# A sorted-block attention and Fourier-mix kernel: three more tile transposes by the DMA crossbar, GpSimd shares an elementwise step, one buffer clear moves, and a new written-out order

## The chip, the cores and the metric

The kernel runs on one core of one Trainium2 chip. The metric is the device time of one launch in microseconds (us). The kernel before the change took 272.64 us, the median of three runs (271.47 to 272.67).

The core has five instruction streams: PE (TensorE, the matmuls, with its weight loads listed as PEld), DVE (VectorE), ACT (ScalarE), POOL (GpSimd) and SP (SyncE, which here only issues DMAs). POOL computes and also issues the loads from HBM. All DMAs of the core, whoever issues them, share 16 DMA engines.

## What is computed

Inputs are q, k, v of shape (4, 8, 768, 64), a sort matrix (4, 8, 8, 8) and two weights (512 x 2048 and 2048 x 512), all float32. Cut to what matters:

```python
P = sinkhorn(sort_net)                      # 5 rounds: exp, row and column normalise
k_sorted = einsum("bhij,bhjcd->bhicd", P, k_blocks)     # 8 blocks of 96 rows
v_sorted = einsum("bhij,bhjcd->bhicd", P, v_blocks)
attn = softmax(q_block @ k_sorted_block.T / 8)
x = attn @ v_sorted_block                   # regrouped to (4, 768, 512)
u = x + real(fft(fft(x, axis=1), axis=2))
un = (u - mean(u)) / sqrt(var(u) + 1e-6)    # over the last axis
out = u + maximum(un @ w_ch1, 0) @ w_ch2
```

## The kernel before

**Tiling and stages.** The four batches run one after the other with much overlap. A batch b has eight heads (four pairs hp) and 768 rows, which are six tiles T of 128 rows. The rows are handled in two halves, g = 0 (tiles 0 to 2) and g = 1 (tiles 3 to 5). Each step is a small Python generator, named by a letter and its indices. The ones that matter here:

- `x` b hp g (L529, L534): scores of two heads on PE, then exp on ACT into an `ex` tile (96 x 384).
- `e` b hp g (L548): one instruction for each of the two heads writes exp minus 1 from `ex` into the padded buffer `eb`. All 64 are on DVE. There are four `eb` buffers.
- `o` b h (L561, L570, L575): attention times values on PE, the reciprocal and the scaling on DVE.
- `f`, `c` (L680 to L739): folds and the first Fourier product. `d` b T (L755, L758, L769): the second one, with two DVE steps into `u`. `p` b T (L776, L782, L784): a copy on ACT, then an add and a subtract on POOL (letter P) or DVE (letter D). `g` b T (L791, L795): mean and variance on DVE. `l` b g (L799 to L808): four small POOL steps that give `ny` and `nm`, the scale and the bias of a half.
- `n` b g tt (L816 or L819, then L825 or L830): the normalized rows `un` (128 x 512, f16, two buffers) by ACT or DVE, and then their transpose into `ut`. In batch 0 this is four PE transposes (L830) and one copy out of PSUM (L286 or L288); in batches 1 to 3 it is one crossbar transpose that SP issues (L825).
- `h` b g fc (L843, L850, L852): the first feed-forward product of a half, 16 groups of four matmuls, each of which reads all of `ut` of that half (128 x 384) and a slice of `w1sb`; then the relu by ACT or DVE.
- `y` b g tt n (L863, L868, L870): the second product, the addition of `u`, and the store by SP.
- `k`, `q`, `v`, `w`, `s`, `M`, `Z`, `a`, `A`, `R`, `r` prepare sorted keys and values, queries, and the correction terms of the transform. `I` issues two matmuls whose result nobody uses.
- `C0`'s steps after the first two have POOL issue the loads of `w1sb` (four, L362) and `w2sb` (four, L365). `L` has POOL load later q and k (L188).

**What sets the order.** A string `ORDER` lists the steps; each mention of a step runs its generator one `yield` further. At the end, every instruction of an engine is tied to the one before it on the same engine, so each of the five streams runs exactly in the written order, POOL's loads and SP's transposes and stores among them. An instruction that waits holds up all that stands behind it on its engine. The letters behind a step choose its engines. A second string, `SLOTS`, chooses the PSUM bank or the buffer of every tile.

In the order before, half g = 0 of batch 0 is normalized and goes through `h` first, and g = 1 later. Before the loop, DVE clears three of the four `eb` buffers (L246) and POOL the fourth (L258).

Of the kernel before, what the change touches and what calls it, by code (L numbers as in the profile page):

```python
# [18 lines left out]
H = 8  # L19
S = 768  # L20
D = 64
# [85 lines left out]
def kernel(  # L107
# [10 lines left out]
    nc = tc.nc  # L118
# [7 lines left out]
        "00011101 00010234 50671030 12436570 13541602 05240031 63725241 "  # L126
        "61012052 63475001 25314102 06103012 04513222 10030415 11274602 "
        "53130145 36510210 03210302 01560420 33200075 60111221 22340330 "
        "01276225 10173200 00200653 04210013 13610004 56102525 11621110 "
        "65112701 35471623 05243052 00016450 16110470 21112364 21160323 "  # L130
        "61172420 61372041 64161010 20345245 17630010 04176325 11271652 "
        "37261401 05032102 33560171 00310010 00620057 32036401 11017624 "
        "23213156 23520605 43101204 47051106 01110521 03411070 16502411 "
        "02713260 50732415 00274113 52224760 11003511 22104731 00001210 "
        "17315000 14236220 31041230 03107652 01103651 01547162 30400762 "
        "37631401 07521240 11101501 01641320 27614031 54302100 11023201 "
        "50262732 36000054 07001001 51143120 04353542 00117102 16572110 "
        "40111035 60270456 07453147 352041 "
# [27 lines left out]
    def start(ins):  # L166
        return tc.keep_in_program_order(ins)
# [74 lines left out]
    NE = 4  # L242
    eb4 = const.tile([97, NE, 2 * S], F16, name="eb4")
    ebuf = [eb4[:, n, :] for n in range(NE)]
    for n in range(NE - 1):
        nc.vector.memset(ebuf[n][0:96, :], 0.0)  # L246
# [11 lines left out]
    start(nc.gpsimd.memset(ebuf[NE - 1][0:96, :], 0.0))  # L258
# [261 lines left out]
    exs = {}  # L520
# [19 lines left out]
    def t_e(b, hp, g):  # L540
        for h2 in range(2):
            if h2:
                yield
            e = ebuf[(2 * hp + h2) % NE]
            ed = bass.AP(
                tensor=e.tensor, offset=e[:, S * g:S * g + 1].offset,
                ap=[e[0:96, :].ap[0], [224, 4], [1, BLK]])
            nc.vector.tensor_scalar(ed, exs[b, hp, g, h2], -1.0, None,  # L548
                                    op0=ALU.add)
# [261 lines left out]
    def t_n(b, g, tt, eng, e2="A"):  # L811
# [10 lines left out]
        if b > 0:  # L822
            if (b, g) not in uns:
                uns[b, g] = wt([128, 4, GT], F16, "ut", 2)
            nc.sync.dma_start_transpose(  # L825
                uns[b, g][:, :, 128 * tt:128 * tt + 128], un)
            return
# [52 lines left out]
    def t_i():  # L880
# [4 lines left out]
        "C0 I4 I5 M00 M01 M02 M03 J M04 M05 C0 B0 C1 B1 B2 D q00A Z0 "  # L885
        "Z0 s02 k00AA H k01AD Z0 s03 q00 k00 k00 k00 x001 k01 b0 s01 "
        "x000 x001 s04 b0 x000 x000 a0 a0 x001 s05 s00 q01D k01 q02D "
        "k01 k02AA q01 e001 k02 k02 v61A v61 v40A e001 v70A v40 v41D "
        "v50D a0 b1 k02 v41 q02 v30A v30 x010 V x010 x010 V T1 v70 "
        "v20A e010 v20 v50 e000 e000 e010 A0 R0 x011 x021 R0 R0 R0 "  # L890
        "q03D q03 R0 R0 x011 x011 x021 v60D v10A v60 v00A k10AA v10 "
        "e011 e011 x021 k03AA R0 v00 x020 x020 k03 k03 k03 o00 o01 "
        "k10 k10 k10 x020 e021 x030 o00 e020 x030 x030 e021 o02 o01 "
        "o00 o01 o03 o02 o03 x031 q11A r1 C2 C3 r0 r1 e030 o03 e020 "
        "o04 k11AA x031 e031 x031 o05 e030 R0 o04 e031 o04 q11 k11 R0 "
        "o02 o05 k11 q10A q13A q13 v51A o07 o07 o05 q10 v51 M10 o06 "
        "v31A k11 x111 x101 x101 x101 v31 M11 o07 o06 f00 o06 f00 "
        "v21A v01A f01 f01 k13AA e101 x110 f02 k13 f02 M12 M13 e101 "
        "f03 f03 M14 v21 x100 x111 x110 x111 e110 c00 L20 f04 x100 "
        "x110 c00 b1 L30 M15 C0 L20 q20 C0 f05 f05 Z1 v01 C0 e111 "  # L900
        "e110 c01 c01 c02 c00 e111 c01 c02 c03 c04 e100 r0 r0 v71A "
        "k12AA c03 q20 c04 d02 v71 v11A x100 d02 p02P d00 p02 d01 k12 "
        "q12A k12 e100 d00 c03 p00P p01P q12 v11 k13 d02 c04 d00 d01 "
        "Z1 c02 d04 p00 k12 k13 d01 p02 p01 p01 p04P Z1 I1 p00 d05 T2 "
        "g02 g01 p05P x121 x121 x131 x131 a1 o13 o10 a1 x121 g00 g01 "
        "x131 C0 g02 g00 l00 l00 l00 l00 e121 o12 I2 x130 e131 o11 "
        "d04 o12 d05 x130 x130 d05 d04 k20AA n001AA o11 q21 I3 e130 "
        "o11 d03 n001 n002AA n001 L21 n000DD o16 n002 p04 o12 n000 "
        "n000 L21 C0 p04 o16 p05 C0 n002 x120 x120 d03 k20 e130 p03P "
        "o13 s15 e120 o13 h00iA h00fD h00f h00i x120 o10 s10 o10 "  # L910
        "h00jD h00j e121 d03 h00cA h00pA h00hA h00h h00p q21 o16 "
        "h00dA e120 k21AA k21 s13 k21 k20 k20 h00c h00kD e131 s12 s14 "
        "x200 k21 h00oA h00nA s11 o14 x200 h00d x200 h00gA o17 h00aA "
        "h00k h00a h00lA wpA h00g p05 C0 o17 o17 o15 h00mA h00bA g05 "
        "o15 o14 o14 wkA h00l h00b wk h00n h00eA h00e o15 f10 h00o wp "
        "y0010 y0020 e200 g04 x201 x201 L30 x211 x211 p03 p03 g03 f11 "
        "f11 g04 f10 f12 h00m C0 g05 g03 l01 f12 e200 f13 y0021 y0022 "
        "l01 l01 x201 weD wbA wb wgD c10 we y0023 l01 q22 f13 n011DA "
        "e201 c10 f14 woA c11 c11 wo y0000 wjD e211 wj x211 y0001 "
        "n011 n011 c12 wg f15 whA wdA y0011 y0002 c13 c12 wh y0023 "  # L920
        "y0023 r1 n012DD f15 n012 y0012 wlA n012 c13 y0013 wcA q22 "
        "wnD waA wa n010DD n010 wl y0003 n010 wd c14 c14 h01aA wn "
        "y0003 wfD q23 q23 T3 y0013 c10 d11 h01oA h01o wiA h01dD h01d "
        "h01lA h01l y0003 y0013 d10 h01pA wc h01a wi h01p wf h01jD "
        "wmD h01gA wm e201 x210 d10 d10 c11 h01g x210 x210 p10P h01j "
        "d12 h01mA k22AD k22 k22 k22 e210 e210 k23DD q31 k23 k23 "
        "h01cA c13 d11 p12P h01c h01hA h01h p11P k23 h01fA h01f e211 "
        "h01iA d12 h01bD d12 p11 h01m h01i h01kA x230 x231 d11 h01b "
        "p12 p12 p11 g11 g12 g11 g12 x220 h01eA x230 h01e x220 x230 "
        "y0110 o22 x231 e231 o20 h01nD h01n o20 h01k o21 p10 p10 o23 "  # L930
        "o23 o20 L31 x220 L31 g10 g10 o23 y0111 y0112 y0120 a1 l10 "
        "l10 l10 l10 o22 o22 y0121 k31AA c14 n101A k31 q31 e230 e220 "
        "A1 c12 x231 o21 o21 k31 x221 n101 R1 e231 R1 n100A n100 "
        "y0100 y0101 q30 R1 R1 R1 n102A n102 x221 y0113 y0113 d13 "
        "y0102 y0122 R1 R1 e230 y0113 x221 e221 k31 d14 R1 R1 r2 r2 "
        "h10iA h10nA h10i d14 q30 k30DD e221 k30 k30 k30 y0123 r2 "
        "e220 y0123 p14P o27 h10eD h10n h10e h10kD o27 d14 y0123 "
        "y0103 d15 o27 h10aA h10a h10dA h10gA h10g h10bA y0103 h10k "
        "p13D p15P h10cA h10c h10hA h10mA h10m h10d q32 d13 d13 y0103 "
        "h10lA h10h h10jD p13 p14 p14 g14 d15 d15 g14 p15 p15 h10fA "  # L940
        "h10f h10oA o26 g15 p13 g13 g13 g15 l11 l11 l11 h10j o26 "
        "h10pD o26 h10b y1010 l11 o24 o24 y1000 h10l o25 n110D o25 "
        "h10o h10p y1011 x311 x311 x311 x301 f21 o25 f21 y1001 n112A "
        "x301 y1020 y1021 o24 f20 f20 n110 r3 e301 n111D y1002 y1012 "
        "f22 f22 f23 f23 c20 c20 y1013 y1022 q32 x300 x301 x300 x310 "
        "y1023 c21 c21 n112 f24 f25 c23 n111 e311 q33 y1013 y1023 c23 "
        "h11cD c22 f25 y1003 y1003 y1023 y1003 c22 c24 x300 h11c c24 "
        "k32DD k33DA k33 k33 e311 x310 k32 k32 d21 k33 p21P k32 d21 "
        "d21 e300 h11fD h11f h11oA e310 d22 d20 p20P h11lA p22P d22 "
        "d22 c24 h11mA c20 r3 h11kA q33 y1013 d20 h11l h11o p22 p22 "  # L950
        "h11m x310 h11hD h11jA h11j g22 o32 x331 e300 x331 h11bA p21 "
        "h11h x331 h11k g22 o32 h11eA h11iA e310 p20 c23 e301 p21 g21 "
        "h11b o32 h11pD h11aD h11a h11e h11i d20 p20 g20 g20 e331 "
        "x330 g21 l20 l20 l20 l20 h11p x321 h11gA h11g h11dA o31 x321 "
        "o30 o31 o31 e321 x321 h11nA h11d n202A y1110 x330 c22 o33 "
        "h11n y1111 y1112 n202 o33 e330 e331 c21 n201A o33 n201 n200D "
        "n200 r3 y1100 y1101 e321 x320 x320 e320 y1113 y1113 o30 "
# [84 lines left out]
```

## Time and profile before

One execution was profiled. Its own time and the main numbers:

| what | value |
| --- | --- |
| time of the profiled execution | 271.9 us |
| its span in the profile | 270.1 us |
| median of three runs | 272.64 us |
| PE busy | 251.8 us (93%) |
| DVE busy | 196.3 us (73%) |
| ACT busy | 126.0 us (47%) |
| POOL busy | 75.0 us (28%) |
| granted PE clock, mean | 0.994 |
| first `h` matmul starts | 61.84 us |
| last PE matmul ends | 267.4 us |
| crossbar transposes `ut<-un` | 18, median 2.4 us to landing |
| crossbar transposes `qt<-qr` | 8, 2.8 to 9.0 us to landing |

How to read it: the page gives busy time by engine, the span cut in 40 slices, the DMA queues, the chain of work that ended last, and groups of instructions by line. The trace behind it answers for single stretches: who waited for whom, instructions in order of time, busy time by stretch, and for each DMA the time from its issue to its landing. Times count from the span's start. A busy PE isn't PE at its peak, since matmuls are pipelined and their ends are modelled.

### The profile page before, as it was taken

What the parts mean: (1) busy time and instruction counts of PE and PEld (TensorE: products, weight loads), DVE (VectorE), ACT (ScalarE), POOL (GpSimd) and SP (SyncE); (2) the same over time, 40 slices, a digit from 0 to 9 for tenths busy, and PEclk for the clock granted to TensorE, in tenths of its full rate; (3) what the DMA queues carried; (4) which work ended last, traced back from release to release, by engine and by line L of the source; (5) the groups of instructions that cost most, each with busy time, mean ns of one, the idle gap of its engine ahead of it and who ended that gap; (6) DMA issues with size and microseconds to landing.
All of it is one profiled execution on the core that took longest, in us unless ns stands there. A gap on an engine that the chain in (4) does not pass through costs nothing.

```text
span 270.1 us, 6119 instructions
## 1 busy us (share of the span) xinstructions
PE 251.8 (93%) x2440; PEld 156.0 (58%) x2440; DVE 196.3 (73%) x489; ACT 126.0 (47%) x287; POOL 75.0 (28%) x118
## 2 busy tenths in 40 slices
PE   0789889789999999999999999999999999999995
PEld 0268776565666666655656655466466545545554
DVE  6787999989999677867698696458965825912523
ACT  2268889885575477352633555133314312431100
POOL 8922400578730006402220053024200521410000
PEclk9988999999999999999999999999999999999999
DMA  6999999989971231843022310230023023020006
GB/s 120 203 253 203 221 245 235 181 104 178 204 119 39 45 102 29 119 107 101 15 55 52 94 47 12 55 119 1 19 42 116 0 45 132 0 53 8 0 12 223
DMA packets 33138, 26.38 MB, mean 98 GB/s; under 512 B 17395, under 2 KB 28787, under 8 KB 33108
## 3 DMA queue, kind: packets, MB, share of 16 engines
q0 software_dynamic: 11712, 13.63, 30.4%
q1 hardware_dynamic: 21398, 12.36, 17.2%
q8 instruction: 19, 0.31, 0.5%
q14 instruction: 9, 0.07, 0.1%
HBM read 29.00 MB, written 6.29 MB: 131 GB/s over the span
## 4 chain that ended last, share of the span: by engine, by line
PE 77%; DVE 8%; DMA 8%; POOL 2%; ACT 2%; issue 1%; DVEq 0%; SPq 0%; POOLq 0%
PE pf L863 31%; PE pf L843 27%; DMA k<-in_k_dram 6%; PE pf L719 3%; PE pf L561 3%; PE pf L529 2%; DVE eb L548 2%; DMA out_dram<-u 2%; PE pf L755 2%; PE pf L758 1%; DVE u L769 1%; PE pf L486 1%; PE pf L511 1%; PE pf L476 1%; PE pf L615 1%
## 5 line engine op out<-in xcount | busy, mean ns | idle before, releaser
L843 PE MATMUL pf<-ut,w1sb 128*128 128x384 f16 x512 | 89.9, 326 | 0.4 <-DVE hr L850 0.2
L863 PE MATMUL pf<-w2sb,hr 128*128 128x512 f16 (+1 forms) x432 | 88.6, 355 | 0.0
L843 PEld LDWEIGHTS <-w1sb 128*128 128x128 f16 x512 | 48.7, 98 | 31.5 <-issue 0.4
L852 ACT ACTIVATE hr<-pf 128x384 f16<-128x384 f32 x78 | 35.8, 494 | 60.6 <-PE pf L843 60.5
L863 PEld LDWEIGHTS <-hr 128*128 128x128 f16 x432 | 38.5, 98 | 37.7
L782 POOL TENSOR_TENSOR u<-u,bs 128x255 f32<-128x255 f32 x21 | 17.6, 844 | 120.2 <-ACT bs L776 69.1
L868 DVE TENSOR_TENSOR u<-pf,u 128x512 f32<-128x512 f32 (+1 forms) x27 | 17.0, 628 | 29.0 <-PE pf L863 28.9
L534 ACT ACTIVATE ex<-pf 96x384 f32<-96x384 f32 x64 | 28.8, 490 | 10.6 <-PE pf L529 8.0
L850 DVE TENSOR_SCALAR hr<-pf 128x384 f16<-128x384 f32 x50 | 26.3, 547 | 7.7 <-PE pf L843 7.6
L548 DVE TENSOR_SCALAR eb<-ex 96x384 f16<-96x384 f32 x64 | 22.9, 374 | 2.6 <-ACT ex L534 2.4
L769 DVE SCALAR_TENSOR_TENSOR u<-r,pf 128x256 f32<-128x256 f16 x48 | 18.3, 411 | 6.6 <-ACT bs L776 3.2
L784 POOL TENSOR_TENSOR u<-u,bs 128x255 f32<-128x255 f32 x21 | 17.7, 849 | 6.5 <-DVE u L769 6.4
L816 ACT ACTIVATE un<-u,nm,ny 128x512 f16<-128x512 f32 x14 | 11.1, 810 | 17.2 <-POOL nm L808 13.5
L791 DVE BATCH_NORM_STATS2 st<-u 128x6 f32<-128x512 f32 x24 | 16.3, 688 | 3.5 <-POOL u L784 3.1
L286 ACT CAST vsf<-pf 96x512 f16<-96x512 f32 x23 | 16.4, 741 | 3.1 <-PE pf L486 3.1
L575 DVE TENSOR_TENSOR r<-pf,rz 128x384 f16<-128x384 f32 x32 | 17.3, 547 | 0.2
L561 PEld LDWEIGHTS <-eb 97*128 97x128 f16 x384 | 14.9, 97 | 3.7 <-DVE eb L548 0.5
L561 PE MATMUL pf<-vsf,eb 97*128 97x65 f16 x384 | 16.4, 194 | 0.3 <-ACT ex L534 0.2
L733 ACT ACTIVATE y<-pf 128x386 f16<-128x386 f32 x16 | 7.4, 498 | 11.3 <-PE pf L719 11.3
L529 PE MATMUL pf<-qt,ksb 64*128 64x96 f16 x256 | 10.0, 209 | 2.5 <-ACT ksb L286 1.9
L277 PE MATMUL pf<-pack 128*128 128x512 f16 x12 | 4.4, 458 | 8.4 <-DVE pw L324 8.2
L286 ACT CAST ksb<-pf 128x384 f16<-128x384 f32 x23 | 10.5, 484 | 2.3 <-PE pf L511 1.6
(118 smaller groups left out, 302.8 us busy)
## 6 DMA issues: line engine op xcount, KB each, us to landing
out_dram<-u SPq DMA_DIRECT2D x23, 256.0 KB, 2.3
vst<-in_v_dram POOLq DMA_DIRECT2D x4, 768.0 KB, 11.7
q<-in_q_dram POOLq DMA_DIRECT2D x6, 384.0 KB, 13.2
k<-in_k_dram POOLq DMA_DIRECT2D x6, 384.0 KB, 10.6
w1sb<-in_moe_w_ch_dram POOLq DMA_DIRECT2D x4, 512.0 KB, 18.6
w2sb<-in_moe_w_ch_dram POOLq DMA_DIRECT2D x4, 512.0 KB, 8.1
kq<-in_k_dram POOLq DMA_DIRECT2D x2, 384.0 KB, 15.1
kq<-in_q_dram POOLq DMA_DIRECT2D x2, 384.0 KB, 16.2
```

The source lines that it names most:

```text
L286: nc.scalar.copy(dst, src)
L534: nc.scalar.activation(ex.rearrange("p j (c r) -> p j c r", r=6), pss[h2][0:96].rearrange("p j (r c) -> p j c r", c=16), AF.Exp, scale=SCALE)
L548: nc.vector.tensor_scalar(ed, exs[b, hp, g, h2], -1.0, None, op0=ALU.add)
L561: nc.tensor.matmul(po[:, 65 * T:65 * T + 65], e[:, S * g + 256 * tt + 128 * n: S * g + 256 * tt + 128 * n + 128], vsf[:, vi:vi + D + 1], s ...
L575: nc.vector.tensor_tensor(rt[:, :, D * h:D * h + D], po3[:, :, 0:D], rz[:, :, None].broadcast_to([128, 6, D]), op=ALU.mult)
L769: nc.vector.scalar_tensor_tensor(u[:, o:o + 256].rearrange("p (j n) -> p j n", n=2), rts[b][:, T, o:o + 256].rearrange("p (j n) -> p j n", ...
L782: e.tensor_tensor(u[:, 1:256], u[:, 1:256], bs[:, 1:256], op=ALU.add)
L784: e.tensor_tensor(u[:, 257:512], u[:, 257:512], bs[:, 255:0:-1], op=ALU.subtract)
L843: nc.tensor.matmul(ps, w1sb[:, c, 128 * fc:128 * fc + 128], uns[b, g][:, c, :], start=(c == 0), stop=(c == 3))
L850: nc.vector.tensor_scalar(hr[:, fc, :], ps, 0.0, None, op0=ALU.max)
L852: nc.scalar.activation(hr[:, fc, :], ps, AF.Relu)
L863: nc.tensor.matmul(po, hrs[b, g][:, fc, 128 * tt:128 * tt + 128], w2sb[:, fc, cols], start=(fc == 0), stop=(fc == 15))
```

## The change

Four edits are made together.

1. The test in `t_n` is widened: in batch 0 the half g = 1 now also goes through SP's crossbar transpose. Three tiles lose four PE transposes each and one copy out of PSUM; SP gets three more transposes. The half g = 0 of batch 0 stays on PE.
2. `t_e` takes an engine letter for each of its two instructions. By the letters in the new order, 20 of the 64 are on POOL and 44 on DVE.
3. DVE clears two `eb` buffers instead of three before the loop, POOL two instead of one.
4. `ORDER` and `SLOTS` are new throughout. Of the 24 `p` steps, 15 instead of 21 are on POOL; of the 128 relus, 79 instead of 78 are on ACT. In batches 0, 1 and 3 the half g = 1 now goes through `n` and `h` ahead of g = 0. All loads, products and stores are still there, in other places.

```diff
-    for n in range(NE - 1):
+    for n in range(NE - 2):
         nc.vector.memset(ebuf[n][0:96, :], 0.0)
...
-    start(nc.gpsimd.memset(ebuf[NE - 1][0:96, :], 0.0))
+    for n in (NE - 2, NE - 1):
+        start(nc.gpsimd.memset(ebuf[n][0:96, :], 0.0))
...
-    def t_e(b, hp, g):
+    def t_e(b, hp, g, e0, e1):
...
-            nc.vector.tensor_scalar(ed, exs[b, hp, g, h2], -1.0, None,
+            eng = nc.vector if (e0, e1)[h2] == "D" else nc.gpsimd
+            eng.tensor_scalar(ed, exs[b, hp, g, h2], -1.0, None,
                                     op0=ALU.add)
...
-        if b > 0:
+        if b > 0 or g > 0:
             if (b, g) not in uns:
                 uns[b, g] = wt([128, 4, GT], F16, "ut", 2)
             nc.sync.dma_start_transpose(
```

Of the new order, the stretch around the first `h` (the first mention of a step is its first part, for `n` the row step; its second mention is the transpose):

```diff
+        "p03P d05 d03 C0 e111 p05P p04D d05 p04 p04 p03 p03 p05 d05 "
+        "p05 g03 g04 g05 g04 g03 g05 l01 l01 l01 l01 v01 d00 I6 k12AA "
+        "k12 k12 k12 d01 a1 q13A p00P k13 q13 a1 d00 x131 x131 a1 d00 "
+        "x130 x130 k21AA k21 d01 q12A o12 o13 o13 n012D p01P n011A "
+        "e130DD o12 e131DD A1 d01 n012 o16 n011 o12 o13 x131 q12 x130 "
+        "e130 o16 R1 n010D e100 o16 x120 x120 x120 e131 n010 o10 x121 "
+        "C0 e101 x121 k20AA k20 k20 e120DP k21 o17 k21 e121DD o11 "
+        "x121 d02 o14 k20 o10 o17 o17 f11 o10 q21 h01hA o14 R1 R1 R1 "
```

By the streams that come out of it, POOL issues in a row, right behind its tenth `e` instruction (`e110`): a load of `w1sb`, one of k, three more of `w1sb`; then come one `e` instruction, four `p` instructions and the four of `l01`; then one `e`, a load of `w2sb`, one `e`, a second load of `w2sb` and a load of q. DVE's row step of `n010` waits for the transpose of `n012`, whose `un` buffer it takes.

## The prediction

> **What bounds the kernel now.** I read the busy times first, then the stretches of 10 us, the list of who waited for whom on PE, and last the DMAs one by one.
>
> ```profile
> PE 251.8 (93%) x2440; PEld 156.0 (58%) x2440; DVE 196.3 (73%) x489; ACT 126.0 (47%) x287; POOL 75.0 (28%) x118
> ```
>
> ```profile
> 40.00:50.00 10.00, 9.58 (x133) 6.62 (x127) 9.91 (x26) 8.95 (x22) 0.14 (x1) 1.00 1.16 234
> 50.00:60.00 10.00, 8.03 (x139) 5.58 (x139) 9.27 (x28) 8.62 (x24) 8.38 (x13) 1.00 0.85 122
> 60.00:70.00 10.00, 9.01 (x91) 5.54 (x88) 9.97 (x23) 6.55 (x16) 8.30 (x10) 1.00 1.27 180
> 70.00:80.00 10.00, 10.00 (x109) 6.26 (x108) 9.52 (x23) 6.03 (x15) 4.18 (x5) 1.00 1.06 169
> ```
>
> The columns are the stretch, its length, busy us of PE, PEld, DVE, ACT and POOL, then granted PE clock, DMA share and GB/s. PE is full from about 67 us to the last matmul at 267.4. Before that DVE is full (9.3 to 10 of 10) and PE has its gaps: 8.15 us until its first matmul and 7 us after it. So there are two regimes. Up to the first `h` matmul (61.84) the steps that lead there set the pace; from there it is PE's work alone. The time is therefore **the start of the first `h` plus PE's work behind it plus the tail**: 61.84 + 205.5 (to 267.4) + 4.5 (to the profiled execution's own time) = 271.9. The median of the three runs is 0.7 above that execution; I leave that out. What the change does must show as a shift of the first `h` or as less PE work behind it.
>
> **PE's work, step by step.** I counted PE's matmuls ahead of the first `h` in both streams. They are the same but for four groups. Two `o` more (24 matmuls L561, 0.38 each by the chain of waits: 0.76), three half `k` more (18 of L511, 12 per 0.46: 0.70), `A1` more (1.02 + 1.39 in the chain: 2.41), and the 12 transposes L830 of `n00` gone from there (three times 0.41: 1.2). So 3.9 us of work is done ahead that was behind. Behind the first `h`, the 12 transposes of `n01` vanish, the 12 of `n00` arrive: 0. The remainder is 205.5 - 3.9 = 201.6. **Break-even: the new first `h` (`h01`) may start at 61.84 + 3.9 = 65.7.** In all PE has 1.2 us less to do, which is the only sure gain.
>
> **When `h01` can start.** Its rows come from `d`, `p`, `g`, `l01`, `n012`, `n011`, `n010`, then the three transposes. First DVE, which was full. I compared its list up to the third variance step (L795), which ended at 56.22 before (start and length lead each row):
>
> ```profile
> 55.92 0.30 DVE L795 BATCH_NORM_AGGREGATE mv<-st 128x2 f32<-128x6 f32 x3
> ```
>
> ```profile
> 56.32 0.26 POOL L799 TENSOR_SCALAR mv<-mv 128x3 f32<-128x3 f32 x1 [0.52 <-DVE mv L795]
> ...
> 57.93 0.25 POOL L808 TENSOR_SCALAR nm<-nm 128x3 f32<-128x3 f32 x1
> ```
>
> The new list holds 13 `e` less (11 are on POOL by then, 2 come later; 0.34 each where they run alone: -4.4), one clear less (-0.7), one `qr` copy less (-0.3), one copy out of PSUM more (+0.6) and one pair of `p` more (+1.0). Net -3.9, so 52.3. The four POOL steps of `l` took 1.96 (56.22 to 58.18): `nm` is there at 54.3, against 58.2. That is the gain of sharing `e`.
>
> Then the part that I think decides. `n012` on DVE takes 0.57 (mean of L819), SP issues its transpose 0.1 later, it lands after L. `n010` on DVE takes the same `un` buffer, so it waits for that landing; 0.57, 0.1, and again L. `h01` reads all of `ut`: 54.3 + 0.67 + L + 0.67 + L = **55.6 + 2L**. What is queued behind the wait: on DVE the `r`, `e` and `rz` steps of batch 1 and then the relus; on PE everything behind `h01`. Between `n012` and `n010` DVE has only about 2.5 us of other work.
>
> How long is L? The trace has the operation in calm times and a near relative in busy ones:
>
> ```profile
> ut<-un SPq DMA_TRANSPOSE x18, 2.4
> ```
>
> ```profile
> qt<-qr SPq DMA_TRANSPOSE x1, 9.0
> ```
>
> ```profile
> qt<-qr SPq DMA_TRANSPOSE x1, 7.3
> ```
>
> ```profile
> rb<-rr SPq DMA_DIRECT2D x1, 32.0 KB, 6.3
> ```
>
> These are SP's DMAs with us from issue to landing. The 18 `ut` transposes all came after 113 us, where the DMA engines had little to do. `qt` is half as large again and takes 2.8 when alone (at 105.3); issued at 45.9 and about 60 beside the loads of weights, q and k it took 9.0 and 7.3. Even a 32 KB copy took 6.3 to 7.1 at 29 to 39 us, against 1.8 at 120. So a loaded queue adds 4.5 to 6.2 us, whatever the size. Bounds for L: 2.4 and 9.0.
>
> Is the queue loaded at 55? In the new POOL stream the first `w1sb` load stands right behind `e110`. The scores that `e110` needs stand just ahead of `c00` on PE, whose matmuls began at 43.81 before. Exp 0.49 and one POOL `e`: the load goes out at 44 to 45, with k and three more `w1sb` at once: 2.4 MB. At 48 to 50 us the engines moved 210 GB/s, so 11.6 us plus about 2: busy to 57 or 58. `nm` at 54.3 releases POOL for one `e`, two `w2sb` loads and q, 1.4 MB or 6.7 us more, to about 65; two more `w2sb` follow. Before, three `w1sb` loads went out at 30 to 31.5 and were gone by 54.3; the new order issues them 14 us later, into just this stretch. So both transposes meet loads, and I take L = 7.0, between the 32 KB rows and the `qt` rows. `h01` starts at 69.6; 69.6 + 201.6 + 4.5 = **275.7 us**.
>
> The Trainium skill, page "DMA: Bandwidth & Descriptors", section "Queues, rings and completion order", says that each DMA engine serves the queues in turn, packet by packet; one would then expect a transpose beside one busy queue to take about twice its time alone. By that estimate L is 4.8, `h01` starts at 65.2 and the time is 271.3. The `qt` rows (2.8 alone, 7.3 and 9.0 loaded) show more than a doubling, so the rows decide.
>
> **The other edits.** DVE's clear (0.70) ends at the first Sinkhorn step today (3.19), so that chain may start up to 0.7 earlier; it is in the sum above. POOL's added clear (1.77, L258) delays the loads of the next q and k, and is covered by the 4.96 us in which POOL stood idle before L357; without that cover the second v load would be 1.8 late. An `e` on POOL isn't in the trace. Bounds: 0.34 (DVE's) and 2.34 (the longest POOL step, L782 at 68.82). Nearest is POOL's copy of 640 f16 columns, 1.23, so 0.74 for 384. Eleven of them are 8 us in a stretch from 22 to 50 where POOL was nearly idle: 0. Six `p` pairs back on DVE (6.0 us) against 20 `e` gone (7): from 80 us on DVE is at 15 to 91%, 0. One relu more on ACT, at 12 to 69% from 80 us on: 0. SP's three issues (1.2 each) meet a free SP: 0. The tail is again a quarter column, its DVE step (0.29) and a 64 KB store (2.0): 0.
>
> **Rivals.**
>
> 1. **The loads are out of the way: faster.** If the queue is calm, L = 2.4 and 55.6 + 2L = 60.4; then PE's arrival binds. It has 0.76 + 0.70 + 2.41 - 1.2 = 2.7 more to do by then and may win back between 0 and 3.9 us of its gaps by DVE's shorter list: 60.6 to 64.5, middle 62.5, **268.6 us** (266.7 to 270.6). For it: the gaps on PE were mostly DVE's (1.3 for `yr`, 0.4 each for `un`, `pmt`, `vsf`). Against: 2.4 MB issued at 44. It decides where L is under 4.5.
> 2. **Half loaded: no change.** With L = 4.5, as the `qt` at 120.8 took beside a store, `h01` starts at 64.6: **270.7 us**; 5.4 gives 272.5. For it: one transpose might fall into a hole between the `w1sb` and the `w2sb` loads.
> 3. **POOL becomes the bound: slower.** At 2.34 per `e`, eleven are 26 us, and with the 4 us of load issues and 6 of `p` and `l` POOL fills 22 to 54 and `l01` slips by 3 or more: **278.7 us** on top of the loads. It decides from about 2.0 per `e` (32 us less those 10, over 11). Against: POOL's steps are that long only beside DVE's two-input steps.
>
> **How the numbers follow.** Forecast (both transposes loaded, L 5.7 to 9) 0.53; rival 1 0.30; rival 2 0.13; rival 3 0.04. A measurement of this kernel can tell about 0.5% (1.4 us) from no change. Slower is the forecast and rival 3: 0.57; faster is rival 1: 0.30; same 0.13. The forecast's own range is 273.1 (L = 5.7) to 279.7 (L = 9.0). Since rival 1 is too likely to leave out, the range reaches to its lower part: 267.2 to 278.8.
>
> **What would show it.** In the profile after: `nm` of the first half at about 54; the first three `ut<-un` at 6 to 8 us to landing, not 2.4; DVE idle for about 4 us before an L821 `un` with the DMA as releaser; PE idle for several us before the first `h` at 69 to 70; 201 to 202 us of PE without gaps behind it. If the first `h` starts before 65.7, I am wrong about the loads; if `nm` comes after 57, about what `e` on POOL costs DVE; if PE has new gaps after `h01`, about the rest.

## The result and the profile after

The kernel after took **283.93 us** (median of 4 runs, 282.35 to 286.27) against 272.08 us before (271.47 to 272.67): 1.0443 times as long, 95% interval 1.0363 to 1.0522. The forecast was 275.7 us in a range of 267.2 to 278.8. The direction was right, the size was not: 11.9 us more, not 3.8, and outside the range. The profiled execution took 283.98 us, its span is 282.2 us.

First the busy times and the slices of the granted PE clock:

```profile
PE 257.0 (91%) x2428; PEld 158.5 (56%) x2428; DVE 197.5 (70%) x477; ACT 127.4 (45%) x287; POOL 87.9 (31%) x127
...
PEclk9979999985799999996899999999999999999999
```

PE has 12 matmuls less than before and is still busy 5.2 us longer, so the matmuls themselves got slower. The clock row says where: besides the dip near the start, which before has too, there are two, at slices 9 to 11 and 19 to 20, about 61 to 75 us and 129 to 136. The stretches show the same (length; busy us of PE, PEld, DVE, ACT, POOL; clock; DMA share; GB/s):

```profile
50.00:60.00 10.00, 7.98 (x154) 6.86 (x154) 8.34 (x23) 8.44 (x22) 8.55 (x13) 1.00 0.80 145
60.00:70.00 10.00, 3.80 (x49) 3.05 (x49) 7.25 (x20) 1.75 (x5) 5.47 (x7) 0.54 1.29 180
70.00:80.00 10.00, 10.00 (x49) 5.45 (x48) 4.37 (x11) 3.90 (x10) 1.40 (x2) 0.77 0.89 100
120.00:130.00 10.00, 6.61 (x65) 3.55 (x64) 4.48 (x10) 2.62 (x6) 0.00 (x0) 0.96 0.70 120
130.00:140.00 10.00, 10.00 (x84) 5.90 (x83) 8.14 (x17) 4.08 (x10) 6.03 (x7) 0.70 0.42 76
```

Between 60 and 70 us PE worked 3.80 us, where it worked 9.01 before. From 120 to 130 us it has a second hole, in a stretch that was full before. The instructions on both sides of the holes, with the idle time ahead of each and its releaser (POOL's last `l` step, DVE's third row step, then PE):

```profile
54.94 0.27 POOL L810 TENSOR_SCALAR nm<-nm 128x3 f32<-128x3 f32 x1
```

```profile
60.97 0.71 DVE L821 TENSOR_SCALAR un<-u,ny,nm 128x512 f16<-128x512 f32 x1 [1.98 <-DMA ut<-un]
```

```profile
62.20 0.53 PE L512 MATMUL pf<-bdk,k 128*64 128x128 f16 x6 [2.27 <-DVE r L577]
...
69.68 11.63 PE L845 MATMUL pf<-ut,w1sb 128*128 128x384 f16 x56 [4.00 <-DVE vcx L464]
```

```profile
129.70 1.44 PE L845 MATMUL pf<-ut,w1sb 128*128 128x384 f16 x4 [3.39 <-DMA ut<-un]
```

`nm` comes at 55.21 us. The third row step waits for the first transpose, and the first `h` starts at 69.68. The label "DVE vcx L464" on PE's 4.00 us is wrong: in the first experiment below the first `h` starts before those steps. The second hole is the same chain in batch 1, ahead of `h11`: POOL's load of q, 0.4 us behind it the transpose of `n112`, and the row step of `n110` (on ACT here), which takes the same buffer and starts 6 us later:

```profile
118.66 0.86 POOL L188 DMA_DIRECT2D q<-in_q_dram  x1 [0.24 <-issue]
```

```profile
119.03 1.20 SPq L827 DMA_TRANSPOSE ut<-un  x1
```

```profile
124.99 0.81 ACT L818 ACTIVATE un<-u,nm,ny 128x512 f16<-128x512 f32 x1 [4.31 <-issue]
```

The profile gives no landing for that transpose, nor the releaser of this row step; the second and third experiment test both. The first and the third transpose of the first half, in us from issue to landing:

```profile
ut<-un SPq DMA_TRANSPOSE x1, 5.0
...
ut<-un SPq DMA_TRANSPOSE x1, 7.8
```

**The account.** From the first `h` (69.68) to PE's last matmul (279.63) are 209.95 us. Forecast for this part was 201.6. The second hole takes 3.39. Half clock takes 2.37 from the 56 matmuls L845 (11.63 where the same 56 take 9.26 in the experiment with fillers) and 3.16 from those at 129.7 to 137.5 (each row there against its length at full clock). 201.6 + 3.39 + 2.37 + 3.16 = 210.5, 0.6 more than measured; the other gaps of PE in this part, 0.6 in all, are left out. So the start of the first `h` explains 4.0 us of the loss (69.68 against the break-even 65.7), a second stall 3.4 and the halved clock 5.5.

### The profile page after: what moved, and what is told of

It reads as the page before. It is cut to its first block, busy times and chain, and to the rows that moved or that the text cites. A ratio compares the mean times of both kernels' runs of the same rounds, so it can differ in the third digit from the quotient of the medians.

```text
span 282.2 us, 6107 instructions
## 1 busy us (share of the span) xinstructions
PE 257.0 (91%) x2428; PEld 158.5 (56%) x2428; DVE 197.5 (70%) x477; ACT 127.4 (45%) x287; POOL 87.9 (31%) x127
## 4 chain that ended last, share of the span: by engine, by line
PE 65%; DMA 13%; DVE 11%; ACT 4%; POOL 4%; issue 3%; SPq 0%; DVEq 0%; ACTq 0%; POOLq 0%
PE pf L845 30%; PE pf L865 19%; DMA ut<-un 6%; DMA vst<-in_v_dram 4%; DMA w2sb<-in_moe_w_ch_dram 3%; PE pf L721 3%; PE pf L563 2%; DVE st L793 1%; PE pf L487 1%; PE pf L757 1%; PE pf L530 1%; PE pf L760 1%; PE pf L512 1%; ACT un L818 1%; POOL ny L805 1%
## 5 line engine op out<-in xcount | busy, mean ns | idle before, releaser
L845 PE MATMUL pf<-ut,w1sb 128*128 128x384 f16 x512 | 94.5, 337 | 7.8 <-DVE vcx L464 4.0
L845 PEld LDWEIGHTS <-w1sb 128*128 128x128 f16 x512 | 50.3, 101 | 42.7 <-issue 13.7
L854 ACT ACTIVATE hr<-pf 128x384 f16<-128x384 f32 x79 | 36.6, 492 | 51.0 <-PE pf L845 50.8
L784 POOL TENSOR_TENSOR u<-u,bs 128x255 f32<-128x255 f32 x15 | 11.3, 753 | 76.6 <-DVE u L771 47.6
L550 POOL TENSOR_SCALAR eb<-ex 96x384 f16<-96x384 f32 x20 | 23.9, 1203 | 33.2 <-ACT ex L535 26.6
L818 ACT ACTIVATE un<-u,nm,ny 128x512 f16<-128x512 f32 x13 | 10.5, 812 | 22.8 <-DMA ut<-un 9.3
L778 ACT COPY bs<-pf 128x256 f32<-128x256 f32 x24 | 8.7, 372 | 24.7 <-PE pf L760 17.3
L563 PEld LDWEIGHTS <-eb 97*128 97x128 f16 x384 | 15.9, 102 | 5.4 <-issue 2.2
L563 PE MATMUL pf<-vsf,eb 97*128 97x65 f16 x384 | 17.3, 200 | 1.6 <-DVE u L771 1.0
L550 DVE TENSOR_SCALAR eb<-ex 96x384 f16<-96x384 f32 x44 | 16.5, 394 | 2.9 <-ACT ex L535 2.8
L801 POOL TENSOR_SCALAR mv<-mv 128x3 f32<-128x3 f32 x8 | 2.6, 320 | 43.3 <-DVE mv L797 43.3
L786 POOL TENSOR_TENSOR u<-u,bs 128x255 f32<-128x255 f32 x15 | 12.0, 804 | 0.0
## 6 DMA issues: line engine op xcount, KB each, us to landing
vst<-in_v_dram POOLq DMA_DIRECT2D x4, 768.0 KB, 11.9
```

The source lines that it names most:

```text
L550: eng.tensor_scalar(ed, exs[b, hp, g, h2], -1.0, None, op0=ALU.add)
L563: nc.tensor.matmul(po[:, 65 * T:65 * T + 65], e[:, S * g + 256 * tt + 128 * n: S * g + 256 * tt + 128 * n + 128], vsf[:, vi:vi + D + 1], s ...
L845: nc.tensor.matmul(ps, w1sb[:, c, 128 * fc:128 * fc + 128], uns[b, g][:, c, :], start=(c == 0), stop=(c == 3))
L854: nc.scalar.activation(hr[:, fc, :], ps, AF.Relu)
```

## The experiments

**Theory A**: the crossbar transposes of a half are chained by the two `un` buffers and land late where POOL's loads start beside them; each stall costs its idle time and then clock. **Theory B**: the three transposes hold one another up, with or without loads. **Theory C**: the transposes aren't it; slow `e` steps on POOL or late steps on DVE hold the first `h`. Theory D, on the clock: it falls for a reason other than PE's idling. In the diffs below, `C0` is the next weight load and `L21`, `L31` are loads of q and k by POOL; entries of `SLOTS` move along with the steps.

### Loads moved away from the first stall

```diff
-x121 C0 e101 ... e121 C0 L21 p01 ... g01 C0 p00 p00 C0 p02 ... p02 g02
+x121 e101 ... e121 p01 ... g01 p00 p00 p02 ... p02 C0 C0 C0 C0 L21 g02
```

> The kernel after, with the four w2sb loads and the q load of batch 2 that stood in GpSimd's stream between 56 and 67 us moved behind the last p step of the half (about 67 us); nothing else differs. Theory A (the crossbar transposes of the first half are slow because they meet these loads, and each stall of PE also costs clock): the transposes land in 2.4 to 3.5 us instead of 5.0 to 7.8, DVE's idle before the third row step goes, the first h starts at 62 to 64.5 instead of 69.7, the half clock from 61 to 74 us shrinks; 275 to 278.5 us against 283.9, the second stall at 126 to 130 stays. Theory B (the three transposes hold one another up, whatever the loads do): the first lands after about 5 still, first h at 66 to 68, 279 to 282 us. Theory C (not the transposes but late steps on DVE, the vcx step L464 that ends at 69.0 or the exp-minus-1 steps on GpSimd, hold the first h): first h stays at 69 to 70, 283 to 285 us.

Measured: 283.63 us (ratio to before 1.0417, 1.0364 to 1.0470). The transposes landed in 2.4 to 2.5 us and the first `h` started at 63.67, though `nm` came 1.1 later than in the kernel after. Of its DMAs (57 to 60 us) and its PE:

```profile
ut<-un SPq DMA_TRANSPOSE x2, 2.5
```

```profile
63.67 2.60 PE L845 MATMUL pf<-ut,w1sb 128*128 128x384 f16 x15
```

```profile
86.73 0.61 PE L487 MATMUL pf<-bdv,vcx 128*128 128x128 f16 x4 [5.20 <-DVE pf L646]
```

```profile
DVE qr L298 <- DMA q<-in_q_dram: 6.7, 1, 6.7
```

The first stall is gone by the loads alone, so A stands and B and C fall for this stall. But the total gained nothing: the second stall stayed, PE waited 1.83 us for `w2sb`, and the q load had been moved too far. A copy of q on DVE waited 6.7 us for it, PE 5.2 us behind that, with half clock after. I expected 275 to 278.5 and had overlooked who reads that load.

### The later q load moved

```diff
-p12D n112 L31 d12 ... h11l p10 h11eA
+p12D n112 d12 ... h11l p10 L31 h11eA
```

> The kernel after, with one load of q for batch 3 (384 KB, issued at 118.7 us) moved to about 130 us, behind the transposes of the second half that stalls; nothing else differs. Theory A: the transpose issued at 119.0 lands in about 3 us instead of 5.5, the row step on ACT starts at about 122.5, the third transpose lands at about 127 instead of 129.6, PE's idle of 3.4 us shrinks to under 1 and the half clock of 129 to 136 goes: -4 to -6.5 us, 277.5 to 280 us. If the store of 256 KB and the qt transpose beside it are what slows it: -1 us or less, 282.5 to 284.5. Theory C says nothing of this stall and expects no change.

Measured: 279.42 us (1.0258, 1.0207 to 1.0309), 4.5 less than the kernel after. The hole ahead of `h11` shrank, and the clock stayed full behind it:

```profile
127.08 0.81 PE L845 MATMUL pf<-ut,w1sb 128*128 128x384 f16 x4 [1.09 <-DMA ut<-un]
```

One 384 KB load issued 0.4 us ahead of a transpose had cost all that. The four matmuls take 0.81 here and 1.44 in the kernel after.

### A third row buffer

```diff
-        un = wt([128, DM], F16, "un", 2)
+        if g == 1 and tt == 0 and b < 2:
+            un = wt([128, 2, 6, 128], F16, "fo", 1, "un")[
+                :, 0, 0:4, :].rearrange("p a w -> p (a w)")
+        else:
+            un = wt([128, DM], F16, "un", 2)
```

> The kernel after, with the row step of the third tile of both stalling halves (n010, n110) writing to memory of its own (borrowed from a fold buffer that is idle then) instead of one of the two row buffers, so that it needn't wait for an earlier transpose to land; the loads stay where they are. Theory A: DVE's idle of 2.0 us before the third row step goes and the third transpose is issued at about 59.5 instead of 61.8; it still meets the loads: landing after 6 to 8, first h at 66 to 67.5 instead of 69.7; in the second stall the third transpose goes out 3 to 4 us earlier and PE's idle of 3.4 us goes with its half clock; in sum -5 to -9 us, 275 to 279 us. If loaded transposes take turns so that the last lands when it did, first h stays at 69 to 70 and only the second stall goes: 278 to 281. Theory C: 283 to 285.

Measured: 279.18 us (1.0248, 1.0202 to 1.0295). First `h` at 67.79, second hole 0.45 us. The wait for the buffer is gone, but the third transpose, issued about 2 us earlier, still met the loads and took 8.2. So at the first stall the buffer is worth 1.9 us of the first `h` and the loads 6.0; at the second either change removes most of the hole.

### Both load moves together

```diff
-x121 C0 e101 ... e121 C0 L21 p01 ... g01 C0 p00 p00 C0 p02 ... n112 L31 d12 ... h11l p10
+x121 e101 ... e121 p01 ... g01 p00 p00 p02 ... p02 C0 C0 C0 C0 L21 ... n112 d12 ... h11l p10 L31
```

> The moves of the first two experiments together (the w2sb and q loads behind the first half's transposes, the later q load behind the second's). Theory A: the sum of both, as the stalls are 60 us apart on a PE that has no gaps between: first h at 62 to 64.5, no idle of PE at 126 to 130, mean granted clock back over 0.98; 269 to 273.5 us. Theories B and C: 278 us or more.

Measured: 280.71 us (1.0312, 1.0275 to 1.0349). First `h` at 63.53, second hole 1.56, but PE waited 1.96 for `w2sb` and 3.68 for the late q load again. The expected sum of both didn't come, for the reason found in the first experiment.

### Loads a little later, and the third buffer

The loads go right behind the last transpose of the half (from 63 us on, q first) instead of at 70; the later q load and the buffer as above.

```diff
-x121 C0 e101 ... e121 C0 L21 p01 ... e120 b1 ... g01 C0 p00 p00 C0 p02
+x121 e101 ... e121 p01 ... e120 L21 C0 b1 ... g01 p00 C0 p00 C0 p02 C0
```

> The kernel after with the causes of both stalls removed: the q load and the four w2sb loads behind the first half's transposes but 5 us earlier than in the first experiment (which made its own stall: a queries copy on DVE waited 6.7 us for the late q load, and PE 5.2 us behind that), the later q load behind the second half's transposes, and the third row steps in memory of their own. Theory A: transposes at 2.4 to 3 us, first h at 62 to 64, no idle of PE over 1 us and no half clock behind it; PE's work behind the first h is about 204 us to the end of the span, so 268 to 271.5 us: level with before or up to 1.5% faster. If something else in the new order costs time behind the first h (theory C), it stays over 274 us though the stalls are gone.

Measured: **273.41 us** (1.0046, 1.0024 to 1.0067), 10.5 us less than the kernel after with the same arithmetic. First `h` at 62.97, no idle of PE over 0.8 us behind it but one of 1.22. Below, it is called the version without stalls.

```profile
62.97 2.76 PE L849 MATMUL pf<-ut,w1sb 128*128 128x384 f16 x16
```

Its load moves and the buffer take back nearly the whole loss, so the two stalls and their clock are nearly all of it. It is some 2 us above what was expected, and slightly slower than before.

### The first edit undone in the kernel after

```diff
-        if b > 0 or g > 0:
+        if b > 0:
...
-A1 d01 n012 o16 n011 o12 o13 x131 q12 x130 e130 ... e131 n010 o10 ... x121 d02 o14
+A1 d01 o16 o12 o13 n012 x131 q12 n011 x130 n012 n011 e130 ... e131 o10 ... x121 n010 d02 n010 o14
```

> The kernel after with the first edit undone: the three tiles of batch 0's second half are transposed on PE again (12 matmuls, three copies on ACT), in the new order, loads and shared exp-minus-1 steps left as they are. Theory A: PE has 1.2 us more to do, but nothing waits for a transpose to land: DVE's idle of 2.0 us goes, first h at 64.5 to 67 instead of 69.7, no or a short half clock; the second stall stays; 277 to 281 us against 283.9. If the crossbar was not what held the first h (theory C): 284 to 286 us, as PE has more work.

Measured: 278.94 us (1.0250, 1.0206 to 1.0295). First `h` at 64.56 with the loads where they were. The second stall was 4.53 here. So it was the crossbar, where it stood, that held the first `h`.

### PE kept busy in its holes

`i` is one matmul whose result nobody uses, a filler.

```diff
-h01hA ... h11lA
+i (12 times) h01hA ... i (15 times) h11lA
```

> The kernel after with PE kept busy in its two idle stretches by matmuls whose result nobody uses: 12 (128x512) ahead of the first h (65.7 to 69.7 us) and 15 ahead of the first h of the second stall (126.3 to 129.7). Nothing else starts earlier. If the half clock behind each stall comes from PE's idling: the clock is full again a few us before the first h and does not fall at 129; 56 matmuls L845 behind the first stall take about 9.3 us instead of 11.6, and the stretch behind the second stall 3 us less; -4 to -6 us, 278 to 280. If the clock falls for another reason (the chip's load, the DMA), it stays at half in the same places and the time stays at 283 to 285 or rises by the fill's excess.

Measured: 284.68 us (1.0467, 1.0431 to 1.0504). Each filler took 0.43 us at full clock, twice my reckoning, so they delayed both `h`. The clock answered all the same:

```profile
67.33 5.58 PE L278 MATMUL pf<-pack 128*128 128x512 f16 x12
72.96 9.26 PE L845 MATMUL pf<-ut,w1sb 128*128 128x384 f16 x56
```

```profile
127.13 6.44 PE L278 MATMUL pf<-pack 128*128 128x512 f16 x15
133.62 0.81 PE L845 MATMUL pf<-ut,w1sb 128*128 128x384 f16 x4
```

The 56 matmuls take 9.26 us, not 11.63, and the four behind the second fill 0.81, not 1.44. With fewer fillers:

```diff
-i (12 times) h01hA ... i (15 times) h11lA
+i (8 times) h01hA ... i (7 times) h11lA
```

> The kernel after with its two idle stretches of PE filled by unused matmuls as before, but fewer (8 and 7 instead of 12 and 15: each took 0.43 us at full clock in the first such run, twice what was reckoned, so that the fill itself ran 3 us too long in both places). If idling causes the half clock: full clock by about 68 us and none lost at 129; the 56 matmuls L845 take 9.3 instead of 11.6 us and the stretch behind 129.7 some 3 us less; 278 to 280.5 us against 283.9. If the stalls alone cost and the clock adds nothing to the time: 283 to 285.

Measured: ratio 1.0359 (1.0294 to 1.0423), against 1.0443 for the kernel after; the intervals overlap. The first fill (66.33 to 70.06) fits, and the 56 matmuls take 9.26 again. The second ended at 127.27, 2.40 us before the transpose landed, and the clock halved there once more. That the half clock follows from PE's idling (against D) is shown by both. That filling pays in time is not shown.

### The first edit alone

In the kernel before, with the third mention of each of the three steps (the copy out of PSUM) dropped from the order:

```diff
-        if b > 0:
+        if b > 0 or g > 0:
```

> The kernel before with only the first edit: the second half of batch 0 through the crossbar, old order, old loads, all exp-minus-1 steps on DVE. In the old order these three tiles come late, behind the first h, where the DMA engines carry little. Theory A: the edit alone is harmless, 12 transposes less on PE: 270.5 to 272 us (0 to -0.6%). If a crossbar transpose stalls this kernel wherever it stands: 274 us or more.

Measured: 272.96 us (1.0035, 1.0018 to 1.0052). Not the small gain expected. Its transposes landed in 2.5 to 3.7 us, but the last of them is now the last thing that `h01` waits for:

```profile
93.25 0.81 PE L843 MATMUL pf<-ut,w1sb 128*128 128x384 f16 x4 [0.72 <-DMA ut<-un]
```

### The sharing of `e`, taken back and alone

Taken back in the version without stalls: all `e` letters ahead of the first `h`, and one of `e120` behind it, to D, but for one of `e110`, so that the `w1sb` loads keep their place behind it:

```diff
-e000DP ... e010DP ... e011PP ... e020PP ... e030DP ... e031DP ... e100PP ... e101DP ... e111DP ... e120DP
+e000DD ... e010DD ... e011DD ... e020DD ... e030DD ... e031DD ... e100DD ... e101DD ... e111DD ... e120DD
```

> The version without stalls (273.4 us) with ten of the eleven exp-minus-1 steps that GpSimd makes ahead of the first h, and one behind, put back on DVE; only e110's stays, so that the weight loads behind it start as they did. If sharing pays as the prediction had it: DVE has 10 times 0.34 more, nm comes at about 58.5 to 59 instead of 55.7, first h at 65 to 67 instead of 63, 275.5 to 277.5 us. If GpSimd's steps slow DVE's beside them as much as they relieve it: nm within 1 us, 272.5 to 274.5.

Measured: 283.58 us (1.0423, 1.0367 to 1.0479), 10 more than the version it starts from, not 2 to 4.

```profile
59.73 0.26 POOL L810 TENSOR_SCALAR nm<-nm 128x3 f32<-128x3 f32 x1
```

```profile
ut<-un SPq DMA_TRANSPOSE x2, 9.9
```

```profile
75.72 2.72 PE L849 MATMUL pf<-ut,w1sb 128*128 128x384 f16 x8 [5.13 <-issue]
```

`nm` came at 59.99 against 55.71: sharing brings `nm` 4.3 us earlier. The rest is the loads once more. The POOL `e` that had held them back until 63 was gone too, so they went out at 62.7 while the rows were 4 us later, and the last two transposes took 9.7 and 10.2 us (the line gives their median). The experiment changed two things, which I had not seen, and its total is no price of sharing; `nm` is.

Alone in the kernel before, with the moved clear and the letters of the kernel after at each `e`:

```diff
-            nc.vector.tensor_scalar(ed, exs[b, hp, g, h2], -1.0, None,
+            eng = nc.vector if (e0, e1)[h2] == "D" else nc.gpsimd
+            eng.tensor_scalar(ed, exs[b, hp, g, h2], -1.0, None,
```

> The kernel before with only the second and third edit: the same 20 exp-minus-1 steps on GpSimd as in the kernel after, one clear moved from DVE to GpSimd, old order and loads, no new crossbar transposes. If sharing pays in itself: nm up to 3 us earlier than 58.2, first h 1 to 2 us earlier than 61.8, 269.5 to 271.5 us. If 1.17 us per step on GpSimd (against 0.34 on DVE) makes the steps behind them late, above all GpSimd's adds of p and the weight loads that stand behind them in the old order: 272 to 276.

Measured: 283.58 us (1.0425, 1.0386 to 1.0464). Above both ranges expected, 269.5 to 271.5 and 272 to 276; the reason is of the second kind, work behind these steps made late, but larger. In the old order two q loads stand behind ten of those `e` on POOL: they went out from 46.46 us instead of at 21.15 and 28.88, a copy of q on DVE waited 4.7 us, PE 5.58 in the same stretch, and the first `h` started at 71.78. Sharing needs the new order: an engine that takes work on also delays the loads that it issues.

### What was left in the version without stalls

First three relus and one row step:

```diff
-h01lD ... h01iD ... h11oD ... n212A c30 c30 f35 f35 c34 c32 c32 c33 n212
+h01lA ... h01iA ... h11oA ... c30 c30 f35 f35 c34 c32 c32 n212A c33 n212
```

> The version without stalls (273.4 us) with three relus moved from DVE to ACT, where PE waited for DVE behind a first h (gaps of 0.73, 0.48 and 0.76 us), and one row step of batch 2 (n212) placed behind four ACT copies that it held up (a gap of 1.22 us). By the list of PE's gaps: 1.5 to 3 us less, 270.5 to 272 us, level with before. If the gaps are only shifted to the next late step: 273 to 274.

Measured: 272.96 us (1.0022, 0.9998 to 1.0045), 0.5 of the 1.5 to 3 us expected, and the intervals of the two versions overlap. A wait of 1.52 us was left ahead of the first `h`, and half clock behind it. On top of this, one DVE step moved ahead of `n012` (and the relu of `h01a` put on ACT):

```diff
-n012D p01P n011A e130DD o12 e131DD A1 d01 n012
+d01 n012D p01P n011A e130DD o12 e131DD A1 n012
```

> The tuned version without stalls (272.96 us) with one DVE step (the second part of d01, L771) moved ahead of the row step n012, into the 0.65 us in which DVE waits for nm, and one more relu on ACT. In the tuned version PE waits 1.52 us (57.4 to 58.9) for that step and runs at half clock from about 61.5 to 64.5 behind it. If the remaining loss sits in that wait: first h at 62 to 63 instead of 64.2, no half clock ahead of it, 270 to 271.7 us, under the kernel before. If PE only waits for the next late step instead: 272.5 to 273.5.

Measured: 271.83 us (1.0003, 0.9983 to 1.0023): level with before. The first `h` starts at 62.16, and all clock is granted (mean 1.0). Beside it, the version with 273.41 us with the first edit undone, by the same lines as above:

```diff
-        if b > 0 or g > 0:
+        if b > 0:
```

> The version without stalls (273.4 us) with batch 0's second half transposed on PE again, so the first edit alone undone where nothing stalls. If a calm crossbar transpose is worth the PE work it saves: 1.2 us slower, 274 to 275.5. If its landing of 2.4 us stays in the chain to the first h: level or faster, 271.5 to 273.8.

Measured: 275.72 us (1.0119, 1.0093 to 1.0146), against 1.0046 with the crossbar: about 2 us slower without the first edit. The prediction counted 1.2 us of PE work for it. The trace of this run also has a new wait of 1.58 us for a transpose ahead of `h11`, so how much of the 2 us is the edit's own is not shown. Then the relus of `h01` in PE's order, and the copy of q for batch 2 later on DVE:

```diff
-o10 q21 h01hA ... h01aA h01a d02 d02 g01 o11 g01 p00 ... h01o h01g h01bA h01dA h01pA ... h01b q21 f11 h01i g00 g00 p02 g02 h01p h01cA h01l
+o10 h01hA ... h01aA d02 d02 g01 o11 g01 h01g h01o q21 p00 ... h01bA h01dA h01l h01a h01pA ... h01b q21 f11 g00 g00 h01p h01i p02 g02 h01cA
```

> The last version (271.83 us, level with before) with the relus of the first h group put on ACT in the order in which PE makes them, and a queries copy on DVE (1.8 us beside GpSimd's DMA issues, 0.35 elsewhere) moved behind the r steps that PE waits for. If the gaps of 0.50, 0.96 and 0.31 us behind the first h are all that is left of the loss, PE has some 1.5 us less idle there: 269.8 to 271 us, 0.4 to 0.8% under the kernel before. If other late steps take their place: 271.3 to 272.3.

Measured: 273.42 us (1.0052, 1.0030 to 1.0075). The `h` group ran without a gap (56 matmuls in 9.26 us from 61.94), but the copy of q that I had put later sent its transpose into the loads at 68.6. It landed after 10.3 us, the next copy on DVE waited 3.44 for it and PE 2.58. Putting that copy ahead of the loads instead:

```diff
-k21 e121DD o11 ... o11 g01 h01g h01o q21 p00
+k21 e121DD q21 o11 ... o11 g01 h01g h01o p00
```

> The version with the relus in PE's order (273.42 us), whose new stall of 2.6 us at 77.6 came from a queries copy made later, so that its crossbar transpose (issued at 68.6) met the weight loads, landed after 10.3 us and held the next copy on DVE, and PE behind it. Here that copy stands 4 us earlier than it ever did (about 61 us), ahead of GpSimd's loads, so that its transpose goes out at 61 to 62 and lands after 3 to 5 us. If that one late landing is what cost 1.6 us: no gap at 77 to 80, 56 matmuls L849 without gaps from 62 us, 269.8 to 271.3 us, under the kernel before. If the next late step takes its place: 271.5 to 273.

Measured: **269.66 us** (0.9914, 0.9890 to 0.9938): 0.9% under the kernel before, 5% under the kernel after, with all four edits in it. The kernel before got no such tuning, so the 0.9% is not the worth of the edits alone. Its stretches, in the columns of above:

```profile
60.00:70.00 10.00, 9.93 (x108) 6.52 (x105) 9.77 (x27) 7.29 (x18) 7.95 (x10) 1.00 0.78 127
70.00:80.00 10.00, 10.00 (x79) 5.89 (x78) 8.49 (x21) 4.86 (x10) 3.74 (x6) 1.00 1.24 200
120.00:130.00 10.00, 9.70 (x131) 6.17 (x130) 9.04 (x22) 7.02 (x17) 6.20 (x9) 1.00 0.72 104
130.00:140.00 10.00, 9.79 (x80) 5.24 (x78) 8.17 (x23) 3.79 (x9) 2.40 (x4) 1.00 0.36 61
```

```profile
62.80 9.26 PE L849 MATMUL pf<-ut,w1sb 128*128 128x384 f16 x56
```

PE is nearly full in all four, at full clock, and the same loads run beside it (127 and 200 GB/s): they are behind the transposes now.

## Why the prediction was right in direction and wrong in size

- **The two regimes.** "From there it is PE's work alone" is the step that failed. PE's work was sized well: the last version goes from its first `h` (62.80) to its last matmul (265.45) in 202.65 us with 1.55 of idle in it, 0.72 of that ahead of one `h`; the forecast was 201.6 without gaps. But it isn't alone. The new order put a q load at 118.66 us, 0.4 ahead of the transpose of `n112`, and that half stalled as the first did. I had examined the loads at one place and let the 18 calm transposes of before (2.4 us) stand for all later ones. The sign named for it ("if PE has new gaps after `h01`, about the rest") is what happened.
- **The clock** was missing from the sum. The trace of before showed it falling behind PE's idle time (0.57 at 18 to 22 us, behind a gap of 1.25 at 17.2), and I gave a stall of several us its idle time only. It cost 5.5 us here, more than the stalled first `h` itself.
- **The start of the first `h`**: forecast 69.6, measured 69.68. The picture was right, but that the sum fits to 0.1 is luck, as the parts were off each way: `nm` at 55.21, not 54.3; the landings 5.0 and 7.8, not 7.0 twice; the row steps 0.7. The estimate of twice the calm time, 4.8, fits the first landing and not the third.
- **What loads the queue** was half wrong. The `w1sb` loads went out 3 us earlier than I had them and were done. From 55 to 57 us the engines moved 35 GB/s. The `w2sb` and q loads issued at 56.3 to 59.2 made the landings late; moving these alone gave 2.5.
- **`e` on POOL**: 0.74 taken, 1.17 measured (20 took 23.9 us). That was covered, as costed at nothing, in the new order, and not in the old one. DVE's list came out 0.8 later than reckoned (53.1 for 52.3); 0.1 of that is the sum itself, whose terms give -3.8, not -3.9.
- **Rivals.** Rival 1 was the right picture of a calm queue: with the loads moved L was 2.4 and the first `h` came at 61.9 to 64.2 in the seven versions that had the loads moved and kept the first edit and the shared `e` (forecast 60.6 to 64.5). Its 268.6 us took four more rounds of moves behind the version without stalls to come near (269.66). Rival 3 didn't happen: POOL was never the bound, at 1.17 an `e`.
- **The range** held no case with a second stall or a lost clock, so 283.9 lay outside it. Its upper end, 278.8, was also below the forecast's own 279.7 for L = 9.0.

Still open: why the label of the first wait names a DVE step, what decides whether a gap halves the clock, and how much of the 5.5 us a correctly sized filler would win back in time.

## What to carry to other kernels

A short DMA on the critical path is priced by what else is issued within a few us of it, and this must be looked up for every place where it stands, not for the first. When an engine that issues loads takes over compute, list each load behind the new work and who reads it: moving a load of q 14 us later made a stall of 5.2 us in one place, and moving one 11 us later cut a stall from 3.4 to 1.1 us in another. And give a stall of PE its clock as well as its idle time.

## What the runs showed of the hardware

**A crossbar transpose under load.** The same 128x512 f16 transpose landed after 2.3 to 2.5 us with the queue calm and after 4.8 to 10.2 in the first half of batch 0 beside loads of 384 to 512 KB; the larger `qt` took 2.7 calm and up to 15.1 loaded (with `e` shared alone).

**The clock doesn't follow the length of a gap.** A gap of 3.39 us (after, at 126.3) and one of 2.40 (fillers) halved it. One of 3.49 in the first experiment at the same place didn't. Behind a gap of 1.52 us that ended at 58.92 it halved in one version (0.63 and 0.52 in the two stretches from 60 to 64 us, so by these means at about 60.5, with PE at work again), and behind one of 1.53 in its sibling it didn't. Once half, it came back 4.2 to 6.3 us after PE was busy again (in the kernel after resumed at 69.68, full by about 74.5; at 129.70, by about 136; with fewer fillers at 63.03, by about 67.2). Of the kernel after (columns as above):

```profile
128.00:130.00 2.00, 0.30 (x2) 0.16 (x3) 0.00 (x0) 0.00 (x0) 0.00 (x0) 0.78 0.59 168
...
134.00:136.00 2.00, 2.00 (x8) 0.94 (x7) 1.97 (x2) 0.95 (x2) 2.00 (x3) 0.51 0.96 98
136.00:138.00 2.00, 2.00 (x28) 1.15 (x27) 1.95 (x4) 0.86 (x2) 1.33 (x2) 1.00 0.65 99
```

The Trainium skill, page "TensorE: Matmul & The Clock Gate", section "What's actually happening", states a free-running window of about 3.4 us that halves the clock after an idle window and restores it after a busy one. A window that isn't tied to the gap would fit gaps of like length with different outcomes; no run tests it. The halving after gaps of 1.5 and 2.4 us and the slower return are not in that rule; here the measurement decides.

**DVE beside POOL.** The same copy of q (128x768, f16 to f16) took 0.35 us while POOL was idle and 1.81 while POOL issued loads; the first from the last version, the other two lines from the version without stalls:

```profile
61.45 0.35 DVE L298 COPY qr<-q 128x768 f16<-128x768 f16 x1
```

```profile
63.38 1.81 DVE L298 COPY qr<-q 128x768 f16<-128x768 f16 x1
```

```profile
63.27 0.87 POOL L188 DMA_DIRECT2D q<-in_q_dram  x1
64.13 0.77 POOL L366 DMA_DIRECT2D w2sb<-in_moe_w_ch_dram  x1
```

The slow copy began 0.11 us behind the issue of a load. In the kernel after the copy began 0.03 us ahead of one and took 0.41. A row step on DVE took 1.40 us beside an `e` on POOL and 0.50 with POOL idle, both in the first experiment.

The Trainium skill, page "SBUF — State Buffer", section "Who interferes with whom", says that DVE copies and tensor-scalar steps can share a port pair with POOL, and that whoever issues first holds it for the whole instruction while the other waits. The times here agree with it; that the port pair is the cause is not shown by a run.
